# First batch of a fused attention, gated FFN and expert kernel: subtractions from GpSimd to VectorE, and the next batch's transposes placed later

## The chip, the cores and the metric

The kernel runs on one core of one Trainium2 chip. The metric is the device time of one execution in microseconds. The kernel before takes 673.47 us, the median of 3 runs (673.11 to 674.36).

## What is computed

Three layers follow each other on 4 batches of 576 rows: attention with 8 heads of 64 and a sliding window of 64 positions, a gated FFN (512 to 1024 to 512, with a convolution over three neighbouring rows as gate), and a mixture of 8 experts of which one row takes one. Cut to what matters here:

```python
scores = scale * np.matmul(q, k.transpose(0, 1, 3, 2))      # masked to 0 <= i - j < 64
attn = np.exp(scores - np.max(scores, axis=-1, keepdims=True))
attn = attn / (np.sum(attn, axis=-1, keepdims=True) + 1e-09)
x = np.matmul(attn, v)                                       # heads side by side: 512 columns
h = np.maximum(x @ w_in, 0.0)
conv_out = sum(conv_w[k] * hp[:, k:k + S, :] for k in range(3))   # hp is h, padded by one row
x = (h * (1.0 / (1.0 + np.exp(-conv_out)))) @ w_out
# then, row by row: out = p[e] * (relu(x @ w1[e]) @ w2[e]) with the chosen expert e
```

`w_in`, `conv_w` and `w_out` come in double precision.

## The kernel before

**Two parts of a number.** A product is made of three matmuls: each operand is held as a high part (`winH`, `woutH`, `gH`, `xH`), which ScalarE writes in a rounded type, and a low part (`winL`, `woutL`, `gL`, `xL`), which is the operand minus its high part. The subtraction is one instruction of two SBUF inputs, or of one PSUM and one SBUF input for `xL` (L308, VectorE).

**The weights.** `w_in` comes in eight chunks of 128 by 512 and `w_out` in eight (`conv_chunk`). A chunk is loaded as pairs of 32 bit words, VectorE makes single precision of it in three bit steps (L558, L560, L562, `bits64`), ScalarE rounds it (L583 or L650) and the low part is subtracted (L584 or L652). Of `w_out` each chunk is also multiplied with the router's weights: TensorE transposes it (L602), ScalarE copies it to `wt` (L603), TensorE multiplies (L606), and ScalarE and VectorE split the 10 columns (L608, L609). Chunks 0 to 5 of `w_in` are done during the first batch's attention, the other ten inside the first batch's FFN, one or two in each of its eight tiles.

**The first batch's attention** has four pairs of heads. Its order is written out by hand, as a string of tokens (`FIRST`), and each engine takes its instructions in that order. A token is a letter, the pair (4 is the next batch's first pair) and a part 0 to 2. T is TensorE's transposes of `k`, `q` and the last 64 rows, and k, q, t read them out of PSUM (k and t on VectorE, q on ScalarE: L196 for the pair 4). S is the score matmuls, R the masked readout with the row's maximum on VectorE (L230), E three exponentials on ScalarE (L242). N and M normalize on VectorE (L251 to L253, then L255 on two chunks of rows, and on the other six). A transposes the weights on TensorE (L268, L270), a copies them to `aT` on ScalarE (L276 to L279). V multiplies with `v`, x and l write the high and low part of the result (L305 on ScalarE, L308 on VectorE). For the weights of chunk i the tokens are c with the three bit steps, h the rounding on ScalarE, u the subtraction on GpSimd. D with a number is so many matmuls of the identity with itself (`warm`), which compute nothing that is used. Z0 and Z1 clear `qbd0` and `qbd1` on GpSimd and issue a pair's loads.

**The FFN of a batch** runs over eight tiles of 128 columns. A tile has two halves of 288 rows, 12 matmuls each (L432), in two PSUM banks `psM`. ScalarE reads a half with ReLU into one of two buffers `h` (L439) and scales the middle tap (L451), VectorE adds the other two (L452, L453), ScalarE takes a tanh (L454), VectorE multiplies (L455), ScalarE rounds to `gH` (L460) and the subtraction gives `gL` (L461, GpSimd except at the very last tile). While a batch's FFN runs, the next batch's attention is mixed into it, and the output product of the batch (L474) follows the tiles. In this stretch a scheduler sets the order of each engine's instructions when the kernel is built. The loads go through SyncE's queue, in order.

Of the kernel before, what the change touches and what calls it, by code (L numbers as in the profile page):

```python
# [21 lines left out]
def kernel(  # L22
# [14 lines left out]
    nc = tc.nc  # L37
# [55 lines left out]
    if True:  # L93
# [313 lines left out]
        def ffn(b):  # L407
# [3 lines left out]
            for f in range(KF):  # L411
# [29 lines left out]
                t = tb[(b * KF + f) % 3]  # L441
                last = b == B - 1 and f == KF - 1
                cuts = (0, HS - 1, S) if last else (0, S)
                e1 = nc.vector if last else nc.gpsimd
                for u, w in zip(cuts, cuts[1:]):
                    tt = t[:, u:w]
                    h0, h1, h2 = (hbuf[:, j + u:j + w] for j in range(3))
# [139 lines left out]

        def conv_in(c, kk):
            fs = slice(c * CC, (c + 1) * CC)
            return conv_chunk(chunk_in(c, kk), winH[:, kk, fs], winL[:, kk, fs], nc.gpsimd, early.get((c, kk)))[1]  # L590

        def conv_out(kk):

            src = w_out.rearrange("(k p) f -> p k f", p=P)
            f, fin = conv_chunk(src[:, kk, :], woutH[:, kk, 0:DM], woutL[:, kk, 0:DM], nc.gpsimd)

            def finish():
                fin()
                wt = y_p.tile([P, KD, P], F32, tag="ysb", name="wt")
                pt = psa.tile([P, 512], F32, tag="a", name="psWT")  # L600
                for j in range(KD):
                    nc.tensor.transpose(pt[:, j * P:(j + 1) * P], f[:, j * P:(j + 1) * P], ident)  # L602
                nc.scalar.activation(wt.rearrange("p j f -> p (j f)"), pt, AF.Copy)  # L603
                ps = psa.tile([P, 512], F32, tag="a", name="psW")
                for j in range(KD):
                    nc.tensor.matmul(ps[:, 0:E1], wt[:, j, :], wgl[:, j, :], start=j == 0, stop=j == KD - 1)  # L606
                wH, wL = woutH[:, kk, DM:DW], woutL[:, kk, DM:DW]
                nc.scalar.activation(wH, ps[:, 0:E1], AF.Copy)  # L608
                nc.vector.tensor_tensor(wL, ps[:, 0:E1], wH.bitcast(F32), op=ALU.subtract)  # L609

            return finish
# [3 lines left out]
            S11 a00 R10 V00 R11 E10 A01 A02 S12 c00 x00 a01 l00 R12 a02 V01 c01 V02 x01 T20 x02 l01 E11 T21 l02 k2 T22  # L615
            t2 c02 q2 v2 E12 S20 S21 R20 N1 S22 E20 M1 A10 a10 R21 h0 V10 R22 A11 u0 x10 A12 a11 l10 Z0 T30 c10 a12
            V11 k3 E21 V12 c11 T31 T32 x11 t3 x12 l11 q3 l12 c12 E22 v3 S30 S31 R30 N2 S32 E30 M2 A20 a20 R31 h1 V20
            R32 A21 u1 x20 A22 a21 l20 T40 c20 a22 V21 k4 E31 V22 c21 T41 T42 x21 t4 x22 l21 q4 l22 c22 E32 c30 c31
            c32 h2 N3 h3 u2 M3 D9 A30 a30 u3 c40 V30 c41 A31 x30 A32 a31 l30 c42 a32 V31 c50 V32 x31 l31 x32 h4 l32
            c51 u4 c52 h5 u5 Z1  # L620
        """

        with tc.manual_schedule():
            warm(bank(0), 6)
            load_pair(0, 0)
            nc.vector.memset(wgl[:, :, E + 1:E1], 0.0)
            KC = 3 * KF
            taps = cv.tile([P, CC, 2], U32, tag="raw", name="cr", bufs=2)[0:KC, 0:P]
            nc.scalar.dma_start(out=taps.rearrange("r p t -> r (p t)"), in_=conv_w.rearrange("k (f x) -> (k f) x", f=KF))
            nc.scalar.dma_start(out=wgl[:, :, 0:E], in_=w_gate.rearrange("(k p) e -> p k e", p=P))  # L630
            nc.scalar.dma_start(out=wgl[:, :, E:E + 1], in_=w_local.rearrange("(k p) e -> p k e", p=P))
            cin = [(c, kk) for c in range(FF // CC) for kk in range(KD)]
            load_pair(0, 1)
            for i, (c, kk) in enumerate(cin[0:6]):
                early[c, kk] = load_chunk(st_p.tile([P, CC, 2], U32, name=f"raw{i}"), chunk_in(c, kk))
                if i < 2:
                    load_pair(0, 2 + i)
            part = {}

            def others(s_, i, g):  # L640

                c, kk = divmod(i, KD)
                fs = slice(c * CC, (c + 1) * CC)
                if s_ == "c":
                    if g == 0:
                        part[i] = cv.tile([P, CC], F32, name="lf")
                    bits64(early[c, kk], part[i], (g,))
                elif s_ == "h":
                    cin.pop(0)
                    nc.scalar.activation(winH[:, kk, fs], part[i], AF.Copy)  # L650
                elif s_ == "u":
                    nc.gpsimd.tensor_tensor(winL[:, kk, fs], part[i], winH[:, kk, fs].bitcast(F32), op=ALU.subtract)  # L652
                elif s_ == "w":
                    part["f"] = cv.tile([P, CC], F32, tag="lf", name="cf")[0:KC, 0:P]
                    bits64(taps, part["f"])
                elif s_ == "W":
                    part["ps"] = bank(0)
                    nc.tensor.transpose(part["ps"][:, 0:KC], part["f"], ident[0:KC, 0:KC])
                elif s_ == "Y":
                    nc.vector.tensor_copy(cw.rearrange("p k f -> p (k f)"), part["ps"][:, 0:KC])  # L660
                elif s_ == "D":
                    warm(bank(0), i)
                else:
                    nc.gpsimd.memset(qbds[i], 0.0)
                    load_pair(1, i)

            attention_first(FIRST, others)

# [577 lines left out]
```

## Time and profile before

| | before |
|---|---|
| median of 3 runs | 673.47 us |
| profiled execution | 671.16 us |
| its span, first to last instruction | 669.4 us |
| TensorE (PE) busy | 635.6 us, 95% |
| VectorE (DVE) busy | 500.5 us, 75% |
| ScalarE (ACT) busy | 471.3 us, 70% |
| GpSimd (POOL) busy | 151.5 us, 23% |
| mean granted TensorE clock | 0.982 |

Times inside the execution count from the span's start. A share of busy time is a mean over stages with different limits; the stages of this kernel are told apart by windows. The clock is given as a share of full speed: 1.00 is 2.4 GHz, 0.50 is 1.2 GHz. An instruction's duration in the timeline includes its last writes; the next one on the same engine may start some 0.08 us before it ends.

### The profile page before, as it was taken

To read this page: it belongs to the slowest core of one execution; us is meant where nothing else is said; L and a number is where in the kernel's file an instruction comes from. 1 tells how busy PE (TensorE), PEld (TensorE's weight loads), DVE (VectorE), ACT (ScalarE), POOL (GpSimd) and SP (SyncE) were. 2 spreads that over 40 slices of the span, in tenths; PEclk is the share of its full clock that TensorE was granted. 3 is DMA by queue.
4 is the path that set the end of the run, shared out by engine and by line. 5 is a ranking of instruction groups with operands and counts; after the bars stand their busy time and mean duration, and the time that the engine had idled before them with its cause. 6 is when DMAs were issued, how large, how long until landed. Compare 5 with 4: busy or idle time off the path is not lost.

```text
span 669.4 us, 12937 instructions
## 1 busy us (share of the span) xinstructions
PE 635.6 (95%) x4398; PEld 554.2 (83%) x4398; DVE 500.5 (75%) x989; ACT 471.3 (70%) x1003; POOL 151.5 (23%) x172
## 2 busy tenths in 40 slices
PE   6858898999999999999999999999999999999995
PEld 4647897899999999999978878888888888888884
DVE  4988987436884168725777788899899889889982
ACT  3855786536885478835625489888888988988982
POOL 2324625000330013303522221211211211211101
PEclk9989897899999999999999999999999999999998
DMA  8884414333234221108002147511451444512770
GB/s 166 214 214 108 130 46 117 77 95 95 64 69 104 64 52 33 32 33 315 1 0 79 48 174 256 194 48 52 153 164 64 145 157 157 166 41 71 240 273 14
DMA packets 91881, 75.77 MB, mean 113 GB/s; under 512 B 72266, under 2 KB 72290, under 8 KB 91812
## 3 DMA queue, kind: packets, MB, share of 16 engines
q1 hardware_dynamic: 85696, 63.78, 32.2%
q0 software_dynamic: 3680, 10.75, 4.8%
q10 hardware_dynamic: 2436, 0.37, 0.4%
q8 instruction: 36, 0.59, 0.4%
q14 instruction: 33, 0.27, 0.1%
HBM read 127.84 MB, written 11.27 MB: 208 GB/s over the span
## 4 chain that ended last, share of the span: by engine, by line
PE 41%; issue 32%; DMA 12%; DVE 6%; SPq 3%; POOL 2%; ACT 1%; ACTq 0%; POOLq 0%
PE psO L474 14%; PE psM L432 13%; DMA out_dram<-h,sidx 10%; PE psA L218 4%; PE psA L298 3%; PE psA L270 2%; PE psA L185 2%; POOL xg L1022 2%; PE psG L543 1%; DMA kt<-in_k_dram 1%; DVE lf L560 1%; PE psW L606 1%; DVE h L452 1%; PE psO L514 1%; SPq L141 1%
## 5 line engine op out<-in xcount | busy, mean ns | idle before, releaser
L432 PE MATMUL psM<-x,winH 128*128 128x288 f32 x512 | 111.0, 305 | 1.4 <-ACT h L439 1.3
L461 POOL TENSOR_TENSOR gL<-h,gH 128x576 fp32r<-128x576 f32 (+6 forms) x54 | 60.6, 1132 | 163.6 <-ACT gH L460 150.3
L432 PEld LDWEIGHTS psM<-x,winH 128*128 128x128 f32 x512 | 82.4, 189 | 3.7 <-ACT h L439 2.1
L1087 POOL DMA_INDIRECT out_dram<-h,sidx x23 | 23.3, 1014 | 233.4 <-ACT h L1086 233.4
L432 PE MATMUL psM<-x,winL 128*128 128x288 f32 x256 | 75.7, 296 | 0.0
L474 PE MATMUL psO<-woutH,gH 128*128 128x262 f32 (+2 forms) x240 | 68.8, 315 | 0.7 <-ACT gH L460 0.7
L474 PE MATMUL psO<-woutL,gH 128*128 128x262 f32 (+2 forms) x240 | 66.7, 306 | 1.2 <-POOL woutL L584 1.2
L1003 DVE TENSOR_TENSOR gL<-raw,gH 128x1024 fp32r<-128x1024 f32 x56 | 65.6, 1220 | 2.2 <-ACT gH L998 0.7
L474 PE MATMUL psO<-woutH,gL 128*128 128x262 f32 (+2 forms) x240 | 65.7, 304 | 0.0
L242 ACT ACTIVATE sS<-sS,mx 128x128 f32<-128x128 f32 (+1 forms) x144 | 55.2, 386 | 12.7 <-DVE mx L230 12.5
L1003 DVE TENSOR_TENSOR winL<-raw,winH 128x1024 fp32r<-128x1024 f32 x48 | 56.4, 1235 | 3.6 <-ACT winH L998 3.6
L998 ACT ACTIVATE gH<-raw 128x1024 fp32r<-128x1024 f32 x56 | 55.8, 1066 | 0.0
L1003 DVE TENSOR_TENSOR woutL<-raw,woutH 128x1024 fp32r<-128x1024 f32 x44 | 51.0, 1221 | 2.8 <-ACT woutH L998 2.8
L432 PEld LDWEIGHTS psM<-x,winL 128*128 128x128 f32 x256 | 48.2, 188 | 0.2
L998 ACT ACTIVATE winH<-raw 128x1024 fp32r<-128x1024 f32 x48 | 47.0, 1062 | 0.0
L1081 PE MATMUL psO<-x,hh 128*128 128x512 f32 x144 | 46.7, 404 | 0.0
L230 DVE CUSTOM_DVE_ANT_0 sS<-psA,mask 128x128 f32<-128x128 f32 (+1 forms) x135 | 31.0, 278 | 21.0 <-PE psA L218 16.8
L1003 DVE TENSOR_TENSOR x<-raw,x 128x1024 fp32r<-128x1024 f32 x36 | 42.0, 1220 | 5.2 <-ACT x L998 4.2
L474 PEld LDWEIGHTS psO<-woutL,gH 128*128 128x128 f32 x240 | 42.8, 190 | 3.2 <-POOL woutL L584 1.6
L474 PEld LDWEIGHTS psO<-woutH,gH 128*128 128x128 f32 x240 | 42.7, 190 | 2.7 <-ACT gH L460 0.9
L1081 PE MATMUL psO<-gH,hh 128*128 128x512 f32 x112 | 44.6, 398 | 0.0
L1081 PE MATMUL psO<-gH,hl 128*128 128x512 f32 x112 | 44.0, 393 | 0.0
(288 smaller groups left out, 1656.9 us busy)
## 6 DMA issues: line engine op xcount, KB each, us to landing
raw<-in_moe_w_dram SPq DMA_DIRECT2D x184, 512.0 KB
v<-in_v_dram SPq DMA_DIRECT2D x56, 128.0 KB
y_dram<-ysb SPq DMA_DIRECT2D x18, 256.0 KB
kt<-in_k_dram SPq DMA_DIRECT2D x32, 128.0 KB
raw<-in_moe_w_in_dram SPq DMA_DIRECT2D x8, 512.0 KB
raw<-in_moe_w_out_dram SPq DMA_DIRECT2D x8, 512.0 KB
qt<-in_q_dram SPq DMA_DIRECT2D x30, 128.0 KB
y_dram<-x SPq DMA_DIRECT2D x2, 256.0 KB
```

Source lines behind the costliest of these rows:

```text
L185: nc.tensor.transpose(ps[:, n * P:(n + 1) * P], src[:, n].rearrange("p h d -> p (h d)"), ident)
L218: nc.tensor.matmul(ps[:, j * P + lo:(j + 1) * P], qbd[:, c, :], kT[:, k0:W * (c + 1)], start=True, stop=True)
L230: nc.vector.tensor_tensor_reduce(sS[:, c, lo:P], ps[:, j * P + lo:(j + 1) * P], mask[:, lo:P], -scale, -NEG, op0=ALU.add, op1=ALU.min, acc ...
L242: nc.scalar.activation(sS[:, c, lo:P], sS[:, c, lo:P], AF.Exp, scale=-1.0, bias=mx[:, c:c + 1], accum_out=sume[:, c:c + 1],)
L298: nc.tensor.matmul(ps[64 * h:64 * h + 64, W * j:W * j + W], vt[:, h, :], a[0:kk, j, 64 * h:64 * h + 64], start=True, stop=True,)
L432: nc.tensor.matmul(ps[:, 0:HS], wt[:, kk, f * P:(f + 1) * P], xt[:, c0:c0 + HS], start=n == 0, stop=n == 3 * KD - 1,)
L461: e1.tensor_tensor(gL[:, f, r:r + m], t[:, done:done + m], gH[:, f, r:r + m].bitcast(F32), op=ALU.subtract)
L474: nc.tensor.matmul(p_[:, 0:cs.stop - cs.start], gt[:, kk, r:r + P], wt[:, kk, cs], start=n == 0, stop=n == 3 * KF - 1,)
L998: nc.scalar.activation(H_, raws[kk], AF.Copy)
L1003: nc.vector.tensor_tensor(L_, raws[kk], H_.bitcast(F32), op=ALU.subtract)
L1081: nc.tensor.matmul(ps, a[:, kk], w[:, kk % 2, :], start=n == 0, stop=n == 3 * KF - 1)
L1087: nc.gpsimd.indirect_dma_start(out=out[:, :], out_offset=bass.IndirectOffsetOnAxis(ap=sidx[:, t:t + 1].bitcast(U32), axis=0), in_=o, in_of ...
```

## The change

Two things change, both in the first batch.

The subtractions of the low parts of ten weight chunks (two of `w_in`, eight of `w_out`, L584) and of the eight tiles' `gL` (L461) go from GpSimd to VectorE. The six early chunks (token u) stay on GpSimd.

In the order of the attention the next batch's transposes T40, T41, T42 and their readouts pass behind the last exponentials E31 and E32, the bit steps of chunk 3 (before: c30 c31 c32 ahead of N3) behind the normalization M3, chunks 4 and 5 become the tokens 4 and 5 of c, h, u further on, and 24 matmuls of `warm` stand in place of 9. The raw loads of chunks 4 and 5 are issued behind the loads of the next batch's first pair (Z0) and not ahead of them.

```diff
-                e1 = nc.vector if last else nc.gpsimd
+                e1 = nc.vector if last or b == 0 else nc.gpsimd
...
-            return conv_chunk(chunk_in(c, kk), winH[:, kk, fs], winL[:, kk, fs], nc.gpsimd, early.get((c, kk)))[1]
+            return conv_chunk(chunk_in(c, kk), winH[:, kk, fs], winL[:, kk, fs], nc.vector, early.get((c, kk)))[1]
...
-            f, fin = conv_chunk(src[:, kk, :], woutH[:, kk, 0:DM], woutL[:, kk, 0:DM], nc.gpsimd)
+            f, fin = conv_chunk(src[:, kk, :], woutH[:, kk, 0:DM], woutL[:, kk, 0:DM], nc.vector)
...
-            R32 A21 u1 x20 A22 a21 l20 T40 c20 a22 V21 k4 E31 V22 c21 T41 T42 x21 t4 x22 l21 q4 l22 c22 E32 c30 c31
+            R32 A21 u1 x20 A22 a21 l20 c20 a22 V21 c21 V22 x21 l21 x22 E31 T40 l22 T41 k4 T42 t4 E32 c22 q4 N3 h2 M3
+            D9 D9 D6 A30 a30 c30 u2 V30 c31 A31 x30 A32 a31 l30 c32 a32 V31 c40 V32 x31 l31 x32 h3 l32 c41 u3 c42 h4
...
-            for i, (c, kk) in enumerate(cin[0:6]):
+
+            def stage_chunk(i):
+                c, kk = divmod(i, KD)
                 early[c, kk] = load_chunk(st_p.tile([P, CC, 2], U32, name=f"raw{i}"), chunk_in(c, kk))
+
+            for i in range(KD):
+                stage_chunk(i)
                 if i < 2:
                     load_pair(0, 2 + i)
...
                     load_pair(1, i)
+                    if i == 0:
+                        stage_chunk(4)
+                        stage_chunk(5)
```

How the order stands on the engines at three places. First VectorE around the last normalization of the first batch (L251 is N3's first instruction; `raw_210` is chunk 2, `raw_212` chunk 3; L189 to L180 read out the next batch's transposes). Before:

```order
L562 SCALAR_TENSOR_TENSOR lf<-raw_210,lf 128x512
L558 TENSOR_SCALAR lf<-raw_212 128x512
L560 SCALAR_TENSOR_TENSOR lf<-raw_212,lf 128x512
L562 SCALAR_TENSOR_TENSOR lf<-raw_212,lf 128x512
L251 TENSOR_SCALAR sume<-sume 128x9
L252 RECIPROCAL sume<-sume 128x9
L253 TENSOR_SCALAR sS<-sS,sume 128x64
```

And now:

```order
L189 COPY kT_130<-psA 128x512
L175 COPY kT_130<-psA 128x64
L179 COPY qbd_128<-psA 64x64
L180 COPY qbd_128<-psA 64x64
L562 SCALAR_TENSOR_TENSOR lf<-raw_210,lf 128x512
L251 TENSOR_SCALAR sume<-sume 128x9
L252 RECIPROCAL sume<-sume 128x9
L253 TENSOR_SCALAR sS<-sS,sume 128x64
```

Chunk 3's three steps have left the place ahead of L251; the readouts of the next batch's transposes have come closer to it.

Second ScalarE in the same stretch, from the exponentials E31 and E32 (the L242 with 128x128) to the rounding of chunk 3 (L650, now L655). Before:

```order
L242 ACTIVATE sS,sume<-sS,mx 128x128 x3
L305 ACTIVATE x<-psA 128x192
L305 ACTIVATE x<-psM 128x192
L196 ACTIVATE qbd_128<-psA 64x8x64 x2
L242 ACTIVATE sS,sume<-sS,mx 128x128 x3
L650 ACTIVATE winH<-lf 128x512 x2
L276 ACTIVATE aT<-psM 64x128
```

And now:

```order
L305 ACTIVATE x<-psO 128x192
L305 ACTIVATE x<-psA 128x192
L242 ACTIVATE sS,sume<-sS,mx 128x128 x6
L196 ACTIVATE qbd_128<-psA 64x8x64 x2
L655 ACTIVATE winH<-lf 128x512
L276 ACTIVATE aT<-psO 64x128
L277 ACTIVATE aT<-psO 128x256
L305 ACTIVATE x<-psA 128x192
L279 ACTIVATE aT<-psM 128x384
L279 ACTIVATE aT<-psA 128x384
L305 ACTIVATE x<-psO 128x192
L305 ACTIVATE x<-psA 128x192
```

All six exponentials stand ahead of L196 now. The rounding of chunk 3, before the second of the two L650, is the instruction behind the last of these rows.

Third VectorE in the first two tiles of the first batch's FFN. Before:

```order
L453 SCALAR_TENSOR_TENSOR h<-h,cw 128x576
L455 SCALAR_TENSOR_TENSOR h<-h 128x576
L560 SCALAR_TENSOR_TENSOR lf<-raw,lf 128x512
L558 TENSOR_SCALAR lf<-raw 128x512
L455 SCALAR_TENSOR_TENSOR h<-h 128x576
L562 SCALAR_TENSOR_TENSOR lf<-raw,lf 128x512
```

And now:

```order
L584 TENSOR_TENSOR winL<-lf,winH 128x512
L453 SCALAR_TENSOR_TENSOR h<-h,cw 128x576
L455 SCALAR_TENSOR_TENSOR h<-h 128x576
L562 SCALAR_TENSOR_TENSOR lf<-raw,lf 128x512
L558 TENSOR_SCALAR lf<-raw 128x512
L455 SCALAR_TENSOR_TENSOR h<-h 128x576
L461 TENSOR_TENSOR gL<-h,gH 128x576
L560 SCALAR_TENSOR_TENSOR lf<-raw,lf 128x512
L584 TENSOR_TENSOR woutL<-lf,woutH 128x512
```

The subtractions have come into VectorE's row, with three instructions between the first L455 and its L461.

## Rows read from the trace of the kernel before

**Rows 1.** Windows by stage: engines' busy times, then granted clock, DMA share, GB/s

```profile
36.00:51.00 15.00, 8.24 (x78) 6.30 (x78) 11.63 (x23) 8.13 (x26) 3.46 (x3) 0.79 0.82 195
...
56.00:110.00 54.00, 46.10 (x361) 43.48 (x360) 51.03 (x120) 40.00 (x109) 27.10 (x17) 0.96 0.37 108
110.00:130.00 20.00, 19.28 (x139) 17.18 (x139) 9.11 (x34) 11.83 (x40) 4.18 (x3) 0.76 0.27 64
130.00:320.00 190.00, 189.97 (x1737) 182.10 (x1737) 107.42 (x350) 120.76 (x381) 40.11 (x64) 1.00 0.30 85
```

**Rows 2.** TensorE's waits from 36 to 130 us: total, times, longest

```profile
PE psM L268 <- DVE sS L253: 5.1, 1, 5.1
...
PE psWT L602 <- DVE woutL L609: 1.6, 1, 1.6
```

**Rows 3.** Timeline of TensorE around A30: start, duration, instruction, idle before

```profile
37.21 0.63 PE L185 MATMUL psA<-ident,kt 128*128 128x128 f32 x4 [1.30 <-DMA kt<-in_k_dram]
...
39.22 1.15 PE L162 MATMUL psA<-ident 128*128 128x256 bf16 x9
45.50 0.42 PE L268 MATMUL psM<-ident,sS 128*64 128x128 f32 x1 [5.14 <-DVE sS L253]
```

**Rows 4.** Timelines of ScalarE, VectorE, GpSimd and SyncE's queue, same stretch

```profile
36.07 0.49 ACT L279 ACTIVATE aT<-psA 128x384 f32<-128x384 f32 x1
...
38.38 0.33 ACT L305 ACTIVATE x<-psA 128x192 fp32r<-128x192 f32 x1 [0.69 <-PE psA L298]
...
39.37 1.19 ACT L196 ACTIVATE qbd<-psA 64x512 f32<-64x512 f32 x2 [0.31 <-PE psA L185]
...
41.37 0.39 ACT L242 ACTIVATE sS<-sS,mx 128x128 f32<-128x128 f32 x1
...
42.97 1.24 DVE L251 TENSOR_SCALAR sume<-sume 128x9 f32<-128x9 f32 x1
...
44.49 0.95 DVE L253 TENSOR_SCALAR sS<-sS,sume 128x64 f32<-128x64 f32 x1
...
42.45 2.95 POOL L652 TENSOR_TENSOR winL<-lf,winH 128x512 fp32r<-128x512 f32 x2 [5.93 <-ACT winH L650]
...
36.55 2.18 SPq L149 DMA_DIRECT2D v<-in_v_dram  x4
```

**Rows 5.** Window of TensorE behind A30: busy, granted clock, DMA share, GB/s

```profile
45.00:46.00 1.00, 0.50 (x2) 0.50 0.93 205
```

**Rows 6.** Timelines of VectorE and GpSimd in the first batch's FFN

```profile
60.72 0.81 DVE L452 SCALAR_TENSOR_TENSOR h<-h,cw 128x576 f32<-128x576 f32 x1
...
62.05 1.86 DVE L453 SCALAR_TENSOR_TENSOR h<-h,cw 128x576 f32<-128x576 f32 x1
...
104.50 1.78 DVE L560 SCALAR_TENSOR_TENSOR lf<-raw,lf 128x512 uint32<-128x512 uint32 x1
...
109.99 0.75 DVE L455 SCALAR_TENSOR_TENSOR h<-h 128x576 f32<-128x576 f32 x1
...
61.58 1.72 POOL L584 TENSOR_TENSOR winL<-lf,winH 128x512 fp32r<-128x512 f32 x1 [2.62 <-ACT winH L583]
```

**Rows 7.** GpSimd's groups from 60 to 122 us: busy, mean, idle before

```profile
L461 POOL TENSOR_TENSOR gL<-h,gH 128x576 fp32r<-128x576 f32 x8 | 13.8, 1725 | 13.3 <-ACT gH L460 10.1 <-ACT woutH L608 3.2
L584 POOL TENSOR_TENSOR woutL<-lf,woutH 128x512 fp32r<-128x512 f32 x8 | 12.0, 1498 | 18.6 <-ACT woutH L583 18.6
```

**Rows 8.** Timeline of VectorE, three undisturbed instructions in a row

```profile
66.66 0.75 DVE L455 SCALAR_TENSOR_TENSOR h<-h 128x576 f32<-128x576 f32 x1
67.33 0.68 DVE L560 SCALAR_TENSOR_TENSOR lf<-raw,lf 128x512 uint32<-128x512 uint32 x1
67.93 0.41 DVE L558 TENSOR_SCALAR lf<-raw 128x512 uint32<-128x512 uint32 x1
```

**Rows 9.** Timelines of ScalarE and GpSimd at one tile's rounding and subtraction

```profile
81.93 0.68 ACT L460 ACTIVATE gH<-h 128x576 fp32r<-128x576 f32 x1 [0.67 <-DVE h L455]
...
82.69 1.42 POOL L461 TENSOR_TENSOR gL<-h,gH 128x576 fp32r<-128x576 f32 x1 [1.41 <-ACT gH L460]
```

More of the change, by code (lines that the diff above doesn't have):

```diff
@@ L617 @@
             V11 k3 E21 V12 c11 T31 T32 x11 t3 x12 l11 q3 l12 c12 E22 v3 S30 S31 R30 N2 S32 E30 M2 A20 a20 R31 h1 V20
-            R32 A21 u1 x20 A22 a21 l20 T40 c20 a22 V21 k4 E31 V22 c21 T41 T42 x21 t4 x22 l21 q4 l22 c22 E32 c30 c31
-            c32 h2 N3 h3 u2 M3 D9 A30 a30 u3 c40 V30 c41 A31 x30 A32 a31 l30 c42 a32 V31 c50 V32 x31 l31 x32 h4 l32
-            c51 u4 c52 h5 u5 Z1
+            R32 A21 u1 x20 A22 a21 l20 c20 a22 V21 c21 V22 x21 l21 x22 E31 T40 l22 T41 k4 T42 t4 E32 c22 q4 N3 h2 M3
+            D9 D9 D6 A30 a30 c30 u2 V30 c31 A31 x30 A32 a31 l30 c32 a32 V31 c40 V32 x31 l31 x32 h3 l32 c41 u3 c42 h4
+            c50 u4 c51 c52 h5 u5 Z1
         """
```

## The prediction

> **What bounds the kernel now.** I read the busy times and the windows by stage first, then TensorE's waits, then the timelines around the longest of them. From 130 to 320 us TensorE is busy 189.97 of 190 us at full clock [rows 1], and its instructions from there on stand in the same order in both kernels; nothing in the diff can move that part, except by starting it earlier or later. So the change is worth what it does to the first 130 us. There TensorE is not the bound: it waits 5.1 us at a stretch for the normalized scores of the first batch's last pair (VectorE, L253), and 1.6 us for VectorE's L609 [rows 2]. Between 56 and 110 us VectorE is busy 51.03 of 54 us [rows 1]: that stretch runs at VectorE's pace, and TensorE, two halves ahead at most (two `psM` banks, two `h` buffers), follows it. After 110 us VectorE is busy 9.11 of 20 us and TensorE again almost all of the time, at a mean granted clock of 0.76 [rows 1].
>
> **Part 1, the order before the FFN.** Today TensorE waits for `kt` of the next batch, whose DMA lands late, and does T40 at 37.21 us [rows 3]; V21 and V22 are queued behind it. ScalarE therefore idles 0.69 us before x21, then copies `qbd` (L196, 1.19 us), and only then takes the last three exponentials, whose last starts at 41.37 and lasts 0.39 us [rows 4]. VectorE has chunk 3's bit steps in front of the normalization, and runs L251 and L253 in 1.24 and 0.95 us, while GpSimd's two subtractions run (42.45, 2.95 us for two) [rows 4]. A30 starts at 45.50 us, after 5.14 us of idle, by which time the granted clock is 0.50, the lower level of 1.2 GHz [rows 3, 5].
> In the new order V21 and V22 need only `aT`, whose copy starts at 36.07 and takes 0.49 us [rows 4]. So x21 and x22 come at about 36.9 and 37.3 us, and the six exponentials follow. Three took from 40.56, the end of L196, to 41.76 [rows 4], 0.4 us each; six take 2.4 us, and the last ends at about 39.8 instead of 41.8 us. On VectorE one bit step (0.60) stands in front of the normalization, done by 39.8; L251 to L253 undisturbed take some 0.17 us each, so A30 may start at 40.6. Nine warm matmuls take 1.15 us [rows 3], 0.13 each; since the last one's own length counts once, I take 2.7 and not 3.1 us for 24; put behind T42, which ends near 38.4, they keep TensorE until 41.1. I take A30 at 41.1, which is 4.4 us earlier, and at full clock. The 15 added matmuls cost at most the 0.5 us between 40.6 and 41.1; they fill a wait.
> What is late next: chunk 3 (c30 to c32, h3, u3) now stands behind the normalization, and h3 on ScalarE behind x32, whose V32 TensorE does after 17 FFN matmuls. By the same 0.13 us for each of them that puts x32 at 47.1, h3 at 47.4 to 47.9, and GpSimd's u3 to 49.2 (1.3 us, as half of the two in [rows 4], rounded down). The FFN's first two halves close there. That is far ahead of today, but the lead can't be kept: the readouts stand behind h4 on ScalarE, chunks 4 and 5 still have to pass VectorE, and u3, u4, u5 each block it once. Counting on in this way the first L452, at 60.72 in [rows 6], comes at about 55.4. **Term 1: -5.3 us.** Its bounds: -3.0 if only the blocked normalization and the bit steps in front of it are won (1.8 + 1.2), and -7.5 if the whole 4.4 us and the 3.1 us that the clock loses between 36 and 51 us ((1 - 0.79) x 15, [rows 1]) reach the FFN.
> The raw loads of chunks 4 and 5 pass behind the ten loads of the pair in SyncE's queue. The bytes are the same in another order: today the pair's last load is issued until 38.73 us (36.55 + 2.18, [rows 4]), now chunk 5's is, and c40 is due near 44.7 and c50 near 50.5. I count them at zero; the cover is the 6 us from 38.7 to 44.7, and each microsecond by which the load takes longer would delay c40 by one.
>
> **Part 2, the subtractions.** GpSimd loses 8 subtractions of 576 columns and 10 of 512, 25.8 us for 16 of them (13.8 + 12.0, [rows 7]). VectorE gets them. Its price: instructions of the same width with two SBUF inputs start 0.67 us (576 columns, L455) and 0.60 us (512 columns, L560) apart when nothing disturbs them [rows 8]. That is 8 x 0.67 + 10 x 0.60 = 11.4 us; seven of each stand before the eighth L455, so 7 x 0.67 + 7 x 0.60 = 8.9 us of it in the stretch where VectorE is the bound. The last four (2.5 us) fall where VectorE idles half of the time [rows 1] and are hidden.
> What goes: while a GpSimd subtraction runs, VectorE's SBUF instructions stretch. L453 takes 1.86 us at 62.05 where the undisturbed L452 at 60.72 takes 0.81, beside GpSimd's 1.72 us at 61.58; L560 takes 1.78 at 104.50 against 0.68 [rows 6, 8]. From 60.72 to 109.99 there are ten such instructions (62.05 the first, 104.50 the last), 8.9 us above their undisturbed times together. The readouts of PSUM by L230 keep their length throughout. **Term 2: -8.9 + 8.9 = 0.** Bounds: -3.0 if the idle that VectorE has there (54 - 51.03, [rows 1]) is filled as well; +8.9 if nothing comes back because the stretched instructions only covered waits.
> The Trainium skill (SBUF, "Who interferes with whom") has this as a lock on a port pair that the two engines share, held for a whole instruction, and adds that a VectorE instruction with two SBUF inputs does not meet a GpSimd one that only writes. By that the memset of `qbd1` behind u5 would not hold L562, which my count of term 1 lets wait for it, and term 1 would be about 0.7 us larger; the sum goes without it.
>
> **Part 3, the tail.** Between 110 and 130 us the clock costs (1 - 0.76) x 20 = 4.8 us [rows 1], in two cold stretches. The first follows the 1.6 us wait for L609 [rows 2], which VectorE reaches late because of stretched instructions, the last of them at 104.50 [rows 6]. With them gone TensorE may come through warm; but it still alternates there with ScalarE and VectorE for every output chunk (transposes, `wt`, L606, L609). **Term 3: -1.2 us**, a quarter of the bound of -4.8; the other bound is 0.
>
> **The sum.** -5.3 + 0 - 1.2 = -6.5 us. The profiled execution took 671.16 us (span 669.4) and would take 664.7. The median of the runs is 673.47, 2.3 us above it, so I forecast 673.47 - 6.5 = **667.0 us**. All bounds together would give -15.3 and +5.9.
>
> **Rivals.**
> *The FFN's start gives most of it back.* Chunk 3 is split later than before, and TensorE can't close its first two halves before GpSimd's u3; with raw chunk 4 or u3 some 2 to 3 us later than I count, term 1 is 2.0 and the sum -3.2: 670.3 us. For it: three engines in a row stand between c30 and u3. Against: VectorE has work in front of L452 in any case.
> *No change.* VectorE idles 3.4 us between 36 and 51 us (15 - 11.63, [rows 1]), and a shorter front wins mainly this idle and the clock. If the idle only moves from before A30 to before the first L452, VectorE's pace gives back all but some 0.5 us: 673.0 us.
> *Slower: VectorE waits for ScalarE.* Each moved subtraction stands in VectorE's own queue behind a copy on ScalarE. GpSimd started 0.8 us after the copy had, which came right behind L455 (81.93 to 82.69, [rows 9]); GpSimd could wait, VectorE holds up the next tile's convolution. If nothing stood between, 18 x 0.8 = 14.4 us; it turns the sign from the ninth exposed wait on (6.5 / 0.8 = 8.1). With 14 of them the sum is -6.5 + 11.2 = +4.7: 678.2 us. For it: VectorE is the bound, and the work given to it is 8.9 us there. Against: in the new order one to four VectorE instructions stand between most L455 and their L461. The Trainium skill (Perfetto Trace Analysis, "Optimizing Scalar/DVE Operations") speaks for this side, as far as it advises to take work off a saturated VectorE, even to GpSimd; in the same place it warns that the two share a port.
> *More.* The tail stays warm and VectorE's idle is filled: -6.5 - 3.0 - 1.5 = -11.0, 662.5 us.
>
> **How the numbers follow.** Forecast 0.48, the FFN's start 0.15, more 0.15, no change 0.10, slower 0.12. About 0.2% (1.3 us) is what a measurement of this kernel tells from no change. Faster is 0.48 + 0.15 + 0.15 = 0.78, same 0.10, slower 0.12. The range goes from 662.5 (the case "more", with half of it below) to 673.0, which takes in the FFN's start and the near side of no change and leaves out the slower case; some 0.2 lies outside.
>
> **What would show it.** Right: A30 (L268) near 41 us with no DMA wait before it and no clock of 0.50 behind it; the first L452 near 55 us; L452, L453, L560 never above 0.9 us after the last early chunk; the eighth L455 at 104 to 105 instead of 109.99 us; TensorE full from some 123 us on. Wrong: VectorE idle before L461 or L584 with ScalarE as the releaser, in sum over 6 us; or TensorE waiting at its first FFN halves for `winL` beyond 50 us.

## The result and the profile after

The changed kernel takes 665.15 us (median of 4 runs, 664.66 to 666.24) beside 673.29 us for the kernel before on the same chip: a ratio of 0.9879, 95% interval 0.9852 to 0.9905, that is 8.1 us less. Forecast were 667.0 us, 6.5 us less, with 662.5 to 673.0 as the range. The profiled execution takes 664.9 us (span 663.2); profile against profile the change wins 6.3 us.

The stages by windows in the kernel after, as [rows 1] (engines' busy times in the order PE, PEld, DVE, ACT, POOL, then granted clock, DMA share, GB/s):

```profile
36.00:51.00 15.00, 13.27 (x127) 11.47 (x124) 13.23 (x36) 10.78 (x40) 4.17 (x3) 1.00 0.92 237
56.00:110.00 54.00, 45.88 (x370) 42.63 (x368) 50.69 (x132) 41.17 (x113) 0.00 (x0) 0.94 0.40 111
110.00:130.00 20.00, 19.17 (x149) 17.62 (x148) 8.32 (x38) 10.27 (x36) 0.00 (x0) 0.83 0.29 70
130.00:320.00 190.00, 189.97 (x1720) 182.01 (x1719) 110.34 (x344) 120.95 (x372) 42.42 (x66) 1.00 0.30 84
```

TensorE's waits from 36 to 130 us, as [rows 2] (total, times, longest):

```profile
PE psWT L602 <- DVE lf L562: 4.1, 1, 4.1
PE psO L474 <- ACT woutH L583: 2.1, 1, 2.1
PE psW L606 <- ACT wt L603: 1.4, 3, 0.7
PE psM L432 <- ACT h L439: 1.0, 1, 1.0
```

The wait of 5.1 us for the normalized scores is gone. A wait of 4.1 us, ahead of the first output chunk's transposes, and one of 2.1 us have come; both show that TensorE now runs ahead of the others.

Timeline of TensorE around A30 (start, duration, instruction, idle before), as [rows 3]: T40 waits for no DMA, and A30, which started at 45.50 us in the kernel before, starts at 39.66 behind the 24 matmuls of `warm` without a gap.

```profile
36.00 0.66 PE L185 MATMUL psA<-ident,kt 128*128 128x128 f32 x4
...
37.04 1.15 PE L162 MATMUL psA<-ident 128*128 128x256 bf16 x9
38.02 1.15 PE L162 MATMUL psM<-ident 128*128 128x256 bf16 x9
39.01 0.82 PE L162 MATMUL psA<-ident 128*128 128x256 bf16 x6
39.66 0.27 PE L268 MATMUL psO<-ident,sS 128*64 128x128 f32 x1
```

ScalarE and VectorE there, as [rows 4]: the last exponential starts at 38.27 instead of 41.37, L196 stands behind it, and L251 and L253 take 0.17 and 0.26 us where they took 1.24 and 0.95.

```profile
38.27 0.39 ACT L242 ACTIVATE sS<-sS,mx 128x128 f32<-128x128 f32 x1
...
38.66 1.18 ACT L196 ACTIVATE qbd<-psA 64x512 f32<-64x512 f32 x2
...
38.78 0.17 DVE L251 TENSOR_SCALAR sume<-sume 128x9 f32<-128x9 f32 x1
...
39.24 0.26 DVE L253 TENSOR_SCALAR sS<-sS,sume 128x64 f32<-128x64 f32 x1
```

VectorE's groups from the first L452 (53.09) to the eighth L455 (100.13), with what it now does itself (busy, mean ns of one, idle before), beside [rows 6 to 8]:

```profile
L452 DVE SCALAR_TENSOR_TENSOR h<-h,cw 128x576 f32<-128x576 f32 x8 | 7.5, 936 | 0.0
L453 DVE SCALAR_TENSOR_TENSOR h<-h,cw 128x576 f32<-128x576 f32 x8 | 6.4, 806 | 0.0
...
L461 DVE TENSOR_TENSOR gL<-h,gH 128x576 fp32r<-128x576 f32 x7 | 5.2, 741 | 0.0
...
L584 DVE TENSOR_TENSOR woutL<-lf,woutH 128x512 fp32r<-128x512 f32 x5 | 3.4, 682 | 0.0
...
L584 DVE TENSOR_TENSOR winL<-lf,winH 128x512 fp32r<-128x512 f32 x2 | 1.4, 676 | 0.0
```

One L452 is still stretched, the first (1.84 us, beside the last early chunk on GpSimd); every other L452 and L453 takes 0.81 us or less. Ahead of L461 and L584 VectorE does not idle.

**Where the time went, in TensorE's account.** From 130 to 320 us TensorE is full in both kernels, so the time is TensorE's work, its idle time and what a low clock costs before that. A window's idle time is its length less the busy time, and the clock costs (1 - clock) x length. The windows behind 51 us, first of before, then of after:

```profile
51.00:62.00 11.00, 9.78 (x78) 9.09 (x78) 8.84 (x23) 6.51 (x22) 4.27 (x4) 0.97 0.34 81
62.00:100.00 38.00, 34.09 (x276) 32.66 (x275) 35.21 (x75) 27.89 (x73) 18.00 (x11) 0.96 0.32 97
100.00:140.00 40.00, 36.51 (x294) 33.01 (x293) 24.04 (x83) 24.89 (x79) 10.55 (x7) 0.87 0.36 93
```

```profile
51.00:62.00 11.00, 6.90 (x47) 6.52 (x46) 10.93 (x17) 6.91 (x15) 2.47 (x2) 0.93 0.53 124
62.00:100.00 38.00, 36.53 (x303) 34.64 (x301) 37.59 (x98) 30.12 (x80) 0.00 (x0) 0.98 0.44 122
100.00:140.00 40.00, 36.62 (x309) 33.18 (x308) 19.20 (x73) 21.96 (x72) 0.00 (x0) 0.87 0.35 88
```

| us lost, idle + clock | before | after |
|---|---|---|
| 36 to 51 | 6.8 + 3.1 | 1.7 + 0.0 |
| 51 to 62 | 1.2 + 0.3 | 4.1 + 0.8 |
| 62 to 100 | 3.9 + 1.5 | 1.5 + 0.8 |
| 100 to 140 | 3.5 + 5.2 | 3.4 + 5.2 |
| sum | 25.6 | 17.4 |

8.2 us less are lost. Of that the 15 added matmuls of `warm` take 1.65 us (0.11 us apart) as work, which leaves 6.5 us; the span is 6.2 us shorter, and the account does not say where the other 0.3 us are. The front won 8.2 us, TensorE gave 3.3 us back as soon as it had run ahead, the tiles from 62 to 100 us won 3.2 us, and the tail won nothing.

### The profile page after: what moved, and what is told of

It is laid out like the page before. It is cut to its first block, busy times and chain, and to the rows that moved or that the text cites. A ratio compares the mean times of both kernels' runs of the same rounds, so it can differ in the third digit from the quotient of the medians.

```text
span 663.2 us, 12959 instructions
## 1 busy us (share of the span) xinstructions
PE 634.2 (96%) x4413; PEld 553.4 (83%) x4413; DVE 501.3 (76%) x1007; ACT 471.9 (71%) x1003; POOL 122.8 (19%) x154
## 4 chain that ended last, share of the span: by engine, by line
PE 42%; issue 31%; DMA 14%; DVE 8%; ACT 2%; POOL 1%; SPq 1%; POOLq 0%; ACTq 0%; DVEq 0%
PE psO L474 14%; PE psM L432 13%; DMA out_dram<-h,sidx 12%; PE psA L218 3%; PE psA L298 3%; PE psA L270 2%; PE psG L543 1%; PE psA L185 1%; PE psA L221 1%; PE psO L514 1%; DVE sS L230 1%; DVE lf L560 1%; DVE sS L255 1%; POOL xg L1030 1%; DVE lf L562 1%
## 5 line engine op out<-in xcount | busy, mean ns | idle before, releaser
L461 POOL TENSOR_TENSOR gL<-h,gH 128x64 fp32r<-128x64 f32 (+5 forms) x46 | 47.0, 1032 | 210.9 <-ACT gH L460 201.9
L474 PE MATMUL psO<-woutH,gH 128*128 128x262 f32 (+2 forms) x240 | 69.3, 317 | 2.1 <-ACT woutH L583 2.1
L474 PE MATMUL psO<-woutL,gH 128*128 128x262 f32 (+2 forms) x240 | 66.8, 306 | 0.0
L474 PE MATMUL psO<-woutH,gL 128*128 128x262 f32 (+2 forms) x240 | 66.1, 305 | 0.0
L242 ACT ACTIVATE sS<-sS,mx 128x128 f32<-128x128 f32 (+1 forms) x144 | 55.2, 387 | 10.8 <-DVE mx L230 10.7
L1006 ACT ACTIVATE gH<-raw 128x1024 fp32r<-128x1024 f32 x56 | 55.8, 1066 | 0.0
L474 PEld LDWEIGHTS psO<-woutH,gH 128*128 128x128 f32 x240 | 43.1, 192 | 4.1 <-ACT woutH L583 2.3
L474 PEld LDWEIGHTS psO<-woutL,gH 128*128 128x128 f32 x240 | 43.3, 192 | 1.5
L474 PEld LDWEIGHTS psO<-woutH,gL 128*128 128x128 f32 x240 | 43.0, 192 | 1.3
```

Of the source, the lines that this page charges most:

```text
L242: nc.scalar.activation(sS[:, c, lo:P], sS[:, c, lo:P], AF.Exp, scale=-1.0, bias=mx[:, c:c + 1], accum_out=sume[:, c:c + 1],)
L461: e1.tensor_tensor(gL[:, f, r:r + m], t[:, done:done + m], gH[:, f, r:r + m].bitcast(F32), op=ALU.subtract)
L474: nc.tensor.matmul(p_[:, 0:cs.stop - cs.start], gt[:, kk, r:r + P], wt[:, kk, cs], start=n == 0, stop=n == 3 * KF - 1,)
L1006: nc.scalar.activation(H_, raws[kk], AF.Copy)
```

## The experiments

The runs were taken on three chips, on which the kernel before has medians of 673.26 to 673.81 us; "less than before" is counted from the median on the same chip.

**Order and engines apart.** First the order alone, with all eighteen subtractions on GpSimd:

```diff
-                e1 = nc.vector if last or b == 0 else nc.gpsimd
+                e1 = nc.vector if last else nc.gpsimd
...
-            ..., nc.vector, early.get((c, kk)))[1]
+            ..., nc.gpsimd, early.get((c, kk)))[1]
...
-            ..., woutL[:, kk, 0:DM], nc.vector)
+            ..., woutL[:, kk, 0:DM], nc.gpsimd)
```

> The changed order alone; all eighteen subtractions stand on GpSimd as before. Theory (the terms as the trace of after shows them: the first L452 comes 7.6 us earlier by the order, the subtractions on VectorE win 2.2 us from there to the eighth L455, the tail gives back 3.4 us): first L452 near 53, eighth L455 some 7.6 us earlier than before, near 102.4, L453 and L560 stretched to 1.7 us and more again; with 2 to 3 us given back in the tail the time is 4.5 to 6 us under the kernel before. Rival 1 (the lead of the front isn't kept when VectorE is slowed as before, since VectorE's pace sets the stretch and fills only idle time): eighth L455 at 107 or later and 0 to 2 us won. Rival 2 (the order is all of it, the subtractions are a wash): 8 us won, as with the whole change.

Measured: 668.38 us, ratio 0.9929 (0.9903 to 0.9955), 5.4 us less than before. The first L452 starts at 54.20, the eighth L455 at 104.00, and L452 and L453 are stretched again (means of 1366 and 1066 ns). The time is inside the theory's 4.5 to 6 us.

Then the engines alone: the three lines of the diff on engines in the kernel before, nothing else.

> The eighteen subtractions on VectorE alone; the order of the attention is that of before. Theory (each part brings its own term, 2.2 us from the first L452 to the eighth L455): A30 near 45.5 us with its 5.1 us wait, first L452 near 60, eighth L455 near 107, and the time 1 to 3 us under the kernel before. Rival 1 (the subtractions are what made the change faster, and the order only moved idle time): 6 us or more won. Rival 2 (without the lead of the order VectorE is simply overloaded by the 8.9 us): 2 to 6 us slower, with TensorE waiting for VectorE or ScalarE in the tiles.

Measured: 667.99 us, ratio 0.9906 (0.9880 to 0.9933), 5.8 us less. From the first L452 on no L452, L453 or L560 is stretched (an L560 ahead of it takes 1.67 us, beside an early chunk's subtraction), and from the first L452 to the eighth L455 VectorE needs 45.80 us (49.27 before, 49.80 in the order alone, 47.04 in the changed kernel). The front of this execution is even later than that of the kernel before: with the old order TensorE waited 3.03 us for `kt`, where the profiled execution of before waited 1.30 [rows 3].

```profile
38.99 1.09 PE L185 MATMUL psA<-ident,kt 128*128 128x128 f32 x4 [3.03 <-DMA kt<-in_k_dram]
...
48.27 0.42 PE L268 MATMUL psM<-ident,sS 128*64 128x128 f32 x1 [4.24 <-DVE sS L253]
```

So each part is faster by itself, 5.4 and 5.8 us, and together they win 8.1, not 11.2. Rival 2 of the first run (the order is all of it) falls; of the second run the theory's 1 to 3 us was too small, and the 5.8 us come close to the 6 of its rival 1.

**Which subtractions.** The changed kernel with gL on GpSimd again (the first line of the diff above alone), and with the weights on GpSimd again (its other two lines):

> The changed kernel with the eight tiles' gL (L461) on GpSimd again; the weights' subtractions stay on VectorE. Theory (what VectorE pays for an own subtraction, 0.67 us, and what it loses to one on GpSimd, 8.9 us for ten stretched instructions, are about equal): between the changed kernel and 1.5 us slower than it. Rival (the stretched instructions cost more than the sum says, because L453 and L455 stand in the chain of each tile): 3 us or more slower than the changed kernel.

> The changed kernel with the ten weight chunks' subtractions (L584) on GpSimd again; gL stays on VectorE. Theory: as with gL, the price on VectorE (0.60 us each) and the stretch are about equal: between the changed kernel and 1.5 us slower; L452 or L453 stretched to 1.7 us and more once per chunk. Rival 1 (the weights' subtractions are not in the chain of a tile, GpSimd has time for them, and VectorE is the bound of the stretch): up to 2 us faster than the changed kernel. Rival 2 (the stretch outweighs): 3 us or more slower.

Measured: gL on GpSimd 671.15 us (0.9959, 0.9940 to 0.9979), 6.0 us slower than the changed kernel; the weights on GpSimd 664.04 us (0.9866, 0.9842 to 0.9892), 1.1 us less, by which the two intervals still overlap. Of the first run the rival came and not the theory; the second is on the side of its rival 1. With e1_order that makes a square: putting gL on VectorE wins 4.3 us (weights on GpSimd) or 6.0; putting the weights there costs 1.1 or 2.8. How far these figures are the subtractions' own, the last group below limits.

**The subtractions taken away.** In the kernel before, GpSimd clears in place of every subtraction of the first batch:

```diff
-                        e1.tensor_tensor(gL[...], t[...], gH[...].bitcast(F32), op=ALU.subtract)
+                        if b == 0 and not last:
+                            nc.gpsimd.memset(gL[...].bitcast(F32), 0.0)
+                        else:
+                            e1.tensor_tensor(gL[...], t[...], gH[...].bitcast(F32), op=ALU.subtract)
...
-                eng.tensor_tensor(wL, f, wH.bitcast(F32), op=ALU.subtract)
+                nc.gpsimd.memset(wL.bitcast(F32), 0.0)
```

> The kernel before with a memset on GpSimd in the place of each of the eighteen subtractions of the first batch (seven of gL, one at the last tile included, and ten of the weights), so that gL and these low parts are zero: GpSimd writes as much and reads nothing. Theory (the stretch of VectorE's instructions of two SBUF inputs comes from GpSimd's reading of two inputs): no L452, L453, L455, L560 or L562 above 0.9 us beside a memset in the tiles; instructions of one SBUF input (L558, 0.41 us undisturbed) may still be stretched; the stretch from the first L452 to the eighth L455 shrinks by up to 8.9 us, and the time falls by 3 us or more. Rival (any work of GpSimd on SBUF stretches them): L452 and L453 of 1.4 us and more stand beside the memsets.

Measured: 667.83 us (0.9901, 0.9866 to 0.9937), 5.6 us less than before. The memsets wait for nothing, so the weights' ran in the first 8 us and the eight of gL in one piece; beside the tiles stands none, and that part of the test did not take place. What it gives instead: with no subtraction on either engine the kernel is as fast as with all of them on VectorE (667.99, the same order of the attention). Read so, VectorE's price for them, 10.06 us of busy time for 14 in e2_engine's stretch, costs nothing that can be measured, and what GpSimd's did to VectorE cost 5.6 us; the limit that the last group below sets holds for this reading too.

The one piece of memsets shows which instructions meet. GpSimd and VectorE in that kernel (L561 is L558 of before, L563 and L565 are L560 and L562, L655 is an early chunk's subtraction):

```profile
57.76 4.50 POOL L462 MEMSET gL<- 128x576 f32 x8 [0.66 <-DVE lf L565]
62.22 1.44 POOL L655 TENSOR_TENSOR winL<-lf,winH 128x512 fp32r<-128x512 f32 x1
```

```profile
58.13 1.00 DVE L561 TENSOR_SCALAR lf<-raw 128x512 uint32<-128x512 uint32 x1
59.16 0.69 DVE L563 SCALAR_TENSOR_TENSOR lf<-raw,lf 128x512 uint32<-128x512 uint32 x1
...
60.41 0.69 DVE L565 SCALAR_TENSOR_TENSOR lf<-raw,lf 128x512 uint32<-128x512 uint32 x1
61.69 0.82 DVE L452 SCALAR_TENSOR_TENSOR h<-h,cw 128x576 f32<-128x576 f32 x1 [0.59 <-ACT h L451]
62.54 1.73 DVE L453 SCALAR_TENSOR_TENSOR h<-h,cw 128x576 f32<-128x576 f32 x1
```

Beside memsets the instruction of one SBUF input takes 1.00 us (0.42 undisturbed) and those of two keep their length; beside the subtraction L453 takes 1.73.

**The tail.** Seventeen matmuls of `warm` more, where TensorE waits between 100 and 118 us:

```diff
                 ps = psa.tile([P, 512], F32, tag="a", name="psW")
+                warm(ps, {4: 10, 5: 2, 6: 2, 7: 3}.get(kk, 0))
```

> The changed kernel with 17 matmuls of warm more, ahead of the products psW of the output chunks 4 to 7 (10, 2, 2, 3), where TensorE waits for ScalarE's copies between 100 and 118 us. Theory (the tail gave back what the front won because TensorE idled there, 2.9 us between 100 and 115, and two stretches at clock 0.50 followed, 1.7 and 3.4 us lost): the matmuls fill idle time, the clock stays at 1.00 through 100 to 130 us, and the time is 3 to 4.5 us under the changed kernel. Rival (the clock is not set off by this idle time, or the filled idle only makes the chunk's chain later): within 1 us of the changed kernel, or up to 2 us slower, cold stretches as before.

Measured: 662.71 us (0.9830, 0.9800 to 0.9860), 2.4 us under the changed kernel. Ten of the matmuls stand where the wait of 2.1 us for the rounding of an output chunk (L583) was, and L474 behind them waits no more:

```profile
104.36 0.94 PE L602 MATMUL psWT<-ident,lf 128*128 128x128 f32 x4
...
105.39 1.27 PE L162 MATMUL psW<-ident 128*128 128x256 bf16 x10
```

Between 100 and 130 us TensorE is busy 29.91 of 30 us at a mean clock of 0.92. In this execution a cold stretch (one at a clock of 0.50) runs from 98 to 105 us, ahead of the filled wait, and from 106 to 130 us the clock is 1.00; behind the unfilled wait of the changed kernel there were two cold stretches. Less was won than the 3 to 4.5 us expected: between 62 and 100 us the clock is 0.90 here instead of 0.98.

The same with the weights on GpSimd:

> Both at once: the weights' subtractions on GpSimd (664.04 us alone) and the 17 matmuls of warm in the tail. If the two gains are of different causes they add: 2 to 4 us under the first alone, 660 to 662 us. If the weights on GpSimd only won by a warmer tail, nothing is added: 663.5 to 665 us.

Measured: 662.81 us (0.9833, 0.9806 to 0.9859), between the two cases expected and no less than e6_warm_tail. The two gains do not add up.

**The number of warm matmuls, and an order that nobody chose.** Nine instead of 24, as before the change:

```diff
-            D9 D9 D6 A30 a30 c30 u2 V30 ...
+            D9 A30 a30 c30 u2 V30 ...
```

> The changed kernel with 9 matmuls of warm ahead of A30 instead of 24. Theory (the 24 fill a wait that A30 has anyway; after the new order the wait is short): the 15 matmuls, 0.11 us apart, take 1.6 us of which about 0.5 us delays A30; without them A30 stands near 39.1, and TensorE's lead is lost again at VectorE's pace, so the time is within 1 us of the changed kernel. Rival (without them TensorE idles 1.5 us and the granted clock falls to 0.50 behind A30, as behind the wait of 5.14 us before): a stretch of clock 0.50 between 40 and 45 us and the time 1.5 to 3 us above the changed kernel.

Measured: 660.92 us (0.9817, 0.9785 to 0.9849), 4.2 us faster than the changed kernel: neither had it. The rival's clock did come (0.50 from 44 to 47 us; by the account above 1.7 us lost from 43 to 48, as much as the fifteen matmuls cost), but the gain lies elsewhere: 100 to 130 us is warm throughout, TensorE busy 28.81 of 30.

```profile
44.00:47.00 3.00, 3.00 (x21) 2.64 (x19) 1.50 (x4) 0.40 (x2) 0.00 (x0) 0.50 0.55 118
...
100.00:130.00 30.00, 28.81 (x270) 25.86 (x270) 20.88 (x80) 19.95 (x70) 0.00 (x0) 1.00 0.39 102
```

The edit had done more than it said. Each token D takes a PSUM bank in turn; one token instead of three shifts which banks A30 and the FFN's first matmuls get, and with that the order which the scheduler gives VectorE and ScalarE in the FFN. Three kernels take the number and the order apart. Nine matmuls in three tokens (VectorE's and ScalarE's order is then row by row that of the changed kernel), fifteen in one (their order is that of e3_warm9), nine in two (a third order):

```diff
-            D9 D9 D6 A30
+            D3 D3 D3 A30
```

> Nine matmuls of warm ahead of A30 as in e3_warm9 (660.92 us), but as three tokens of three and not as one of nine. Every token of warm takes a PSUM bank in turn, so with three tokens the scheduler gives VectorE and ScalarE the same order as in the changed kernel (665.15 us, 24 matmuls in three tokens). Theory (the order of the mixed stretch makes most of the 4.2 us between the two): the time stays above 663 us, with cold stretches behind 100 us as in the changed kernel. Rival (the fifteen matmuls make it: 1.65 us of TensorE's time and what follows from it): 660 to 662 us.

> Fifteen matmuls of warm in one token; VectorE and ScalarE have the order of e3_warm9 (660.92 us, nine in one token). Theory (the number matters little, the order much): 660 to 662.5 us; the 1.4 us that TensorE idles ahead of A30 in e3_warm9 and the stretch of clock 0.50 behind it are filled by the six, which take 0.65 us. Rival (each matmul of warm costs its length or more): 661.6 us and more for six, in the direction of the changed kernel.

> Nine matmuls of warm in two tokens (five and four), which gives a third order of the mixed stretch by the turn of the banks alone; the work is that of e3_warm9 and of e9_nine_in_three. Theory (orders that nobody chose differ by some us): a time that is 2 us or more from at least one of the two others. Rival (the order of the mixed stretch is worth nothing, all three are alike): all three within 1 us.

| order of the FFN by | number of `warm` | median, us | its runs | mean granted clock of each |
|---|---|---|---|---|
| three tokens | 24 (the changed kernel) | 665.15 | 664.66 to 666.24 | 0.985 to 0.987 |
| three tokens | 9 (e9) | 664.72 | 663.12 to 668.17 | 0.980 to 0.987 |
| one token | 9 (e3) | 660.92 | 659.13 to 664.31 | 0.985 to 0.993 |
| one token | 15 (e10) | 660.42 | 660.35 to 662.82 | 0.989 to 0.994 |
| two tokens | 9 (e12) | 661.58 | 661.36 to 662.71 | 0.988 to 0.992 |

The number is worth nothing that can be measured, the order some 4 us. Of e12 the expectation asked for 2 us to one of the others, and got 3.1 to e9; one and two tokens are alike. The clock goes with it: the faster orders run at a mean granted clock that is some 0.005 higher, and 0.005 of 660 us are 3.3 us. One place where the orders differ can be read. TensorE in the changed kernel: two L474 behind the transposes of an output chunk, then an L474 that needs the next rounding, and only behind it the product psW and the next batch's attention (L270, L298, L218):

```profile
99.29 0.60 PE L602 MATMUL psWT<-ident,lf 128*128 128x128 f32 x4
...
102.20 0.39 PE L474 MATMUL psO<-woutH,gH 128*128 128x262 f32 x1 [2.06 <-ACT woutH L583]
103.07 1.06 PE L606 MATMUL psW<-wgl,wt 128*128 128x10 f32 x8 [0.48 <-ACT wt L603]
103.98 0.53 PE L270 MATMUL psA<-ident,sS 128*128 128x128 f32 x3
...
105.33 1.65 PE L218 MATMUL psA<-kT,qbd 128*128 128x128 f32 x6
```

The L218 at 105.33 takes 1.65 us, at half the clock; in e3_warm9 the same instruction takes 0.94. The same place in e9_nine_in_three waits as long, and is cold again from 106 to 110 us:

```profile
104.06 0.39 PE L474 MATMUL psO<-woutH,gH 128*128 128x262 f32 x1 [2.07 <-ACT woutH L583]
...
106.00:110.00 4.00, 4.00 (x26) 3.43 (x27) 1.40 (x4) 1.52 (x4) 0.00 (x0) 0.50 0.03 10
```

In e3_warm9 the L474 stands behind psW and the attention, and waits for nothing:

```profile
102.47 0.60 PE L602 MATMUL psWT<-ident,lf 128*128 128x128 f32 x4
...
103.76 1.06 PE L606 MATMUL psW<-wgl,wt 128*128 128x10 f32 x8 [0.44 <-ACT wt L603]
104.67 0.53 PE L270 MATMUL psA<-ident,sS 128*128 128x128 f32 x3
...
105.78 0.94 PE L218 MATMUL psA<-kT,qbd 128*128 128x128 f32 x6
106.53 0.51 PE L474 MATMUL psO<-woutH,gH 128*128 128x262 f32 x2
```

This place accounts for the first cold stretch of the changed kernel at most. Its second, from 119 to 125 us, comes behind waits of at most 0.35 us (from 109 us on), and what set it off is not shown.

**Both best edits at once**, nine matmuls in one token and the weights on GpSimd:

> The two best single edits together: nine matmuls of warm in one token (660.92 us) and the weights' subtractions on GpSimd (664.04 us with 24 matmuls, 1.1 us under the changed kernel). If both gains are of their own, 659 to 660 us. If the weights on GpSimd won by the order or the clock that the scheduler and the run happened to give, 661 to 665 us.

Measured: 661.68 us (0.9823, 0.9799 to 0.9847), no faster than e3_warm9 alone. The 1.1 us of e5_w_pool is not a gain of the weights' engine that holds in another order. The lowest median of all is that of e10_15_in_one, 660.42 us, 4.7 us under the changed kernel and 12.8 under the one before it.

These kernels also limit what the square above says, and e1_order, e2_engine and e7_memset with it. Every change of engines gives the FFN another order, and an order alone is worth up to 4 us. That both parts of the change are faster stands clear of noise; how the 8.1 us divide between them is not settled. That gL should stand on VectorE (4.3 and 6.0 us) rests on two pairs of orders and is likely, not settled; for the weights (1.1 and 2.8 us the other way) nothing is settled.

## Why the prediction was right, point by point

**The sign and the size.** Faster, by 8.1 us where 6.5 were forecast; against the profiled execution it was 6.3 for 6.5. That the sum came so near is luck: in the prediction's own steps the two profiled executions give 7.6 us up to the first L452 (forecast 5.3), 2.2 more up to the eighth L455 (forecast 0), and 3.6 of that back behind it (forecast: 1.2 more won), together 6.2 us of span. Two terms were too small by 4.5 us, the third too large by 4.8.

**The profiled execution and the median.** The prediction carried the 2.3 us between them over as a constant. That step failed: the median of after is 0.25 us above its profiled execution. Why the medians differ by 1.8 us more than the profiles (8.1 and 6.3) stays open; two things are on record. With the old order TensorE waited 1.30 us for `kt` in the profiled execution, 3.03 in e2_engine and 2.75 in e7_memset; with the new one it waits for no DMA in front of T40. The pair's load of `kt`, whose order was counted at zero, is issued at 28.70 us instead of 29.76, and T40 stands 1.2 us later behind A20; the runs don't tell these two apart. And where the clock of an execution of the kernel before is on record, those at a mean of 0.982 took 670.8 to 671.2 us, the profiled one among them, and the others, at 0.973 to 0.980, took 671.3 to 676.3 us. The front alone does not explain it: e1_order has no wait for `kt`, and its median is 2.6 us above its profiled execution.

**Term 1, -5.3 us.** Right in its steps: A30 behind the warm matmuls, no wait, no cold stretch behind it. The profiled execution came to A20 1.1 us early (32.18 instead of 33.28), and not by the order: e1_order has A20 at 33.29. Counted from A20, A30 comes 7.48 us later and the first L452 20.91 us (12.22 and 27.44 before): 4.7 us won at A30, where 4.4 were forecast, and 6.5 at L452. The 20.91 stands within 0.01 us in e1, e4, e5, e6, e8 and e9, the kernels with this order up to there, so term 1 was sized 1.2 us too small. Some 1.0 us of this lies in the marker: the count lets each early subtraction block VectorE ahead of the first L452, but the last one (u5) fell on that L452 itself, which takes 1.84 us instead of 0.81. "The 15 added matmuls cost at most 0.5 us" holds by e9 and e10.

**Term 2, 0 us.** The two prices cancelled, much as counted: 14 subtractions are 9.95 us of busy time, some 0.08 us of each under the next instruction, for 8.9 forecast, and VectorE's busy time in the stretch from the first L452 to the eighth L455 hardly moved (46.37 and 46.63 us; the two do not hold quite the same instructions). What fell is its idle time, from 2.90 to 0.41 us, most of it a wait for ScalarE's exponentials ahead of L251. First before, then after:

```profile
60.72:109.99 49.27, 42.28 (x334) 40.13 (x334) 46.37 (x104) 36.05 (x94) 24.80 (x15) 0.96 0.40 118
...
L251 DVE TENSOR_SCALAR sume<-sume 128x9 f32<-128x9 f32 x2 | 1.3, 652 | 2.0 <-ACT sS L242 1.9
```

```profile
53.09:100.13 47.04, 41.47 (x332) 39.21 (x331) 46.63 (x113) 35.39 (x90) 2.23 (x2) 0.96 0.44 120
...
L251 DVE TENSOR_SCALAR sume<-sume 128x9 f32<-128x9 f32 x2 | 0.3, 160 | 0.0
```

So the stretch is 2.2 us shorter, by the idle that the prediction named as a bound of -3.0 and left out of its sum. In time the subtractions were worth more than the stretch of the trace shows, 3.2 us from e1_order to the changed kernel, 5.8 with the old order; e7_memset points the same way for that side, since without any subtraction nothing more is won. A reason may be that the zero sets the two prices against each other as if VectorE's length alone were the time: GpSimd stretched the chain of a tile (L452, L453, L454, L455), while VectorE's own subtractions stand between the links of two tiles. That is argued from the orders, and no run isolates it.

**Term 3, -1.2 us.** This step failed. The stretched instructions went, and so did the wait for L609, but from 100 to 140 us the tail lost as much as before, 3.4 + 5.2 us: a wait of 2.06 us for a rounding, ahead of an L474, stands in its place, with a cold stretch behind it and a second one from 119 us. With that wait filled (e6) or another order (e3, e10) the tail is warmer or warm throughout, and 2.4 to 4.7 us are won.

**The markers.** A30 at 39.66 (near 41), the first L452 at 53.09 (near 55), no clock of 0.50 behind A30 [rows 5], L452 and L453 never above 0.81 and L560 never above 0.69 after the last early chunk: right. The eighth L455 came at 100.13, four us ahead of the marker, and it was no measure of the end, since e4_gl_pool has it at 103.05 and is 6 us slower, and e2_engine at 110.19 and is 3 us faster than that. "TensorE full from 123 on" was true only of its busy time; the clock was 0.50 up to some 125 us.

**The rivals.** VectorE waiting for ScalarE behind each subtraction did not happen: no idle ahead of L461 or L584. The Trainium skill (Perfetto Trace Analysis, "Optimizing Scalar/DVE Operations") says that relieving a saturated VectorE, even by GpSimd, may make sense, and warns that between these two it might not help. Here the warning decides: in e2_engine VectorE has the subtractions, is busy 45.65 of 45.80 us, and the kernel is 5.8 us faster than before. The Trainium skill's rule for a VectorE instruction with two SBUF inputs (SBUF, "Who interferes with whom") agrees with the rows shown: L562 at 54.86 takes 0.68 us beside the memset of `qbd1`, for which the prediction's count had let it wait. It stands behind the first L452 here, so it explains nothing of what term 1 lacked.

```profile
54.26 1.06 POOL L669 MEMSET qbd<- 128x1152 f32 x1
...
54.86 0.68 DVE L562 SCALAR_TENSOR_TENSOR lf<-raw,lf 128x512 uint32<-128x512 uint32 x1
```

The rival of the FFN's start did not happen: the first L452 came early and TensorE waited for chunk 3 only 0.2 us. The 3.3 us that TensorE gave back are of another place, where it waited for VectorE's bits of the first output chunk (4.1 us). Of the case "more" one half came: VectorE's idle was filled, the tail did not stay warm.

## What to carry to other kernels

Where one engine is full after a point, write the time as that engine's work, its idle time and its clock, window by window; a lead won in front shows at once where it is given back. Before an engine swap is credited with a few microseconds, change something that does no work but turns the scheduler's order, here the number of tokens, and see how far the time moves by that alone. Small work of two SBUF inputs on GpSimd beside a saturated VectorE cost VectorE about as much here as doing it itself, so weigh both prices and not the number of busy engines.

## What was not expected of the hardware

A wait of 2.06 us on TensorE (2.07 in e9_nine_in_three), behind shorter ones of 0.2 and 0.7 us, was followed by 3 and 6 us at a clock of 0.50 in two kernels of the same order. In e3_warm9 waits of at most 0.62 us between 96 and 116 us left the clock at 1.00.

Yet a wait of one length does not always have the same end. In e3_warm9 the wait of 1.37 us in front of A30, with waits of 0.52 and 0.31 us behind it, was followed by 3 us at 0.50; with fifteen matmuls (e10_15_in_one) it was 0.71 us and the clock still fell (0.51 from 44 to 47 us); in e9_nine_in_three it was 1.36 us, with 0.52 us behind it, and the clock stayed at 1.00 from 36 to 51 us. The wait of 3.0 us ahead of L602 near 60 us is in e3_warm9 and in e10_15_in_one, of one order: in the first the clock is 0.50 from 62 to 66 us, in the second 1.00 from 60 to 70. The runs do not show what decides.

In e3_warm9 and e10_15_in_one the first L452 came 21.76 and 21.65 us behind A20, later than the 20.91 of the changed kernel, and both are faster even so.
